# Two-layer decode forward and backward on one core: where layer 0's softmax numerators, two K chunks and a weight tile are kept, and when the output rows are written

## The chip, the cores and the metric

The kernel runs on one core of a Trainium2 chip. The metric is device time in microseconds (us) of one execution. Three runs of the kernel before took 1101.24, 1101.69 and 1105.03 us; the median is 1101.69. A fourth execution was profiled; its own time is given below.

The core has TensorE (PE, with its weight loads shown as PEld), VectorE (DVE), ScalarE (ACT), GpSimd (POOL) and SyncE (SP). Here SP issues the loads, POOL the stores, each in order. SBUF is addressed as 128 partitions; sizes below are elements per partition.

## What is computed

Two rounds of attention block and MLP over a KV cache, for one token in each of two batches, with one set of weights used by both rounds, and then the gradient of all inputs but one (`B_x`) for a given `grad_out`. Cut to what matters:

```
B, Sq, D = 2, 1, 1024;  Hq, Hkv, Sk, Dh = 32, 4, 16384, 128;  F = 3584

def A(x, k_cache, v_cache, wq, wo):
    q = (x @ wq).reshape(B, Sq, Hq, Dh).transpose(0, 2, 1, 3)
    k, v = repeat(k_cache, 8, axis=1), repeat(v_cache, 8, axis=1)
    p = softmax(einsum("bhqd,bhkd->bhqk", q, k) * Dh ** -0.5)
    o = einsum("bhqk,bhkd->bhqd", p, v)
    return o.transpose(0, 2, 1, 3).reshape(B, Sq, Hq * Dh) @ wo

def Bm(x, w1, b1, w2, b2):
    return gelu(layernorm(x) @ w1 + b1) @ w2 + b2

def fwd(x, ...):                       # the same weights twice
    x = x + A(layernorm(x), ...);  x = x + Bm(layernorm(x), ...)
    x = x + A(layernorm(x), ...);  x = x + Bm(layernorm(x), ...)
    return x

out, vjp = jax.vjp(fwd, x, k_cache, v_cache, wq, wo, w1, b1, w2, b2)
return out, *vjp(grad_out)
```

`out_0` is the result and `out_1` the gradient of x (2 x 1024 each); `out_2` and `out_3` are the gradients of the two caches (32 MB each in bf16), `out_4` to `out_9` those of the weights and biases.

## The kernel before

**Units.** The cache has eight groups (two batches, four KV heads). A group's K, and its V, is four chunks; a chunk is one tile of 128x4096 bf16 (1024 KB), and a chunk is worked in four slots of eight 128x128 blocks. Weights come in tiles of the same size. The pool `ld` holds seven such tiles in turn; ten more tiles of that size have fixed places (`mid8`, `late8`, `keepV0` to `keepV3` and `keepK0` to `keepK3` for the last group, and `keepxV`, `keepxK`). What is in a fixed place is loaded once and used by later passes: `kv_load` (L518) keeps a table `held`, and `early` (L504) names tiles that stay until a phase: K chunk 2 of group 0 in `mid8` until layer 1's forward pass, V chunk 0 of group 0 in `late8` until layer 1's backward pass.

**Forward pass of a layer** (`attn_layer_fwd`, `attn_fwd`, L612). A slot transposes eight K blocks on PE (`emit_T`, L535), and a copy by ScalarE or VectorE (`evac_bf16`, the one with less charged work) moves them from PSUM into the ring `kT`, four tiles of 128x1024. Two slots later PE forms the scores. After a group's 16 slots come the maximum, then 16 exponentials on ScalarE (`ex`, L654) into `e_all`, a tile of 128x16384 for both layers with layer 0's and layer 1's numerators beside each other (per group: 64 pairs of blocks, 2 layers, 8 heads, 2), and then the products with V (`Acc.quad`, L571).

**Layer order.** Layer 0's attention and MLP, layer 1's attention and MLP (the MLP's w1 tiles fill all seven `ld` buffers and are kept), then backward: `weights_down(1)` (L990: w1's products, then the eight wo tiles through class `Back`), `attn_bwd(1)` (L716, 128 slots, in order of groups), w2's products, `weights_down(0)`, and then the main loop from L1628 on, which does layer 0's attention backward and both layers' cache gradients. `Back.load` (L399) issues a tile's load and queues four units that turn it; `Back.run` turns tile k+1, then multiplies tile k.

**The main loop.** Each step m has two slots that transpose V blocks into the ring `kT`, scores against them, cache gradients (`kv_pair`, L1443: four products into four PSUM banks, four copies, a store) and units from two queues, `fill` and `late` (outer products of the weight gradients; `step_fill`). Operands come as blocks (`make_blks`, L1216: transposed numerators and score gradients) and as spread queries (`q_spread`, `q_make`). The operands of the first chunks are made ahead, in a function that `weights_down(0)` calls after its third w1 tile (`mid`), together with the row of `out_0`: `col_to_row_f32` (L201) turns the eight f32 columns with f32 transposes in one PSUM bank, in two halves, and stores 2 x 1024. The same function writes `out_1` in the tail, behind the last layer-norm backward (`attn_in_bwd`), between the last two `kv_pair` calls.

**Rings.** Besides the transposed K, `columns` (L302) takes a tile of the ring `kT` for the transposed sums at the end of each `Back`. The order on each engine is the order in which the program is written; the framework adds the semaphore waits.

Of the kernel before, what the change touches and what calls it, by code (L numbers as in the profile page):

```python
# [23 lines left out]
def kernel(  # L24
# [60 lines left out]
    ktp = ctx.enter_context(tc.tile_pool(name="ktp", bufs=4))  # L85
# [115 lines left out]
    def col_to_row_f32(colT, J, dram_out, name, home, queue=nc.gpsimd):  # L201
        row = home[0:2].rearrange("p a b -> p (a b)")
        for j0 in range(0, J, 4):
            ps = pm_([2, 4, 128], F32, name)
            for j in range(4):
                PE.transpose(ps[0:2, j, :], colT[:, j0 + j, :], identf[:])
            V.tensor_copy(out=row[:, j0 * 128:(j0 + 4) * 128], in_=ps[0:2, :, :].rearrange("p a b -> p (a b)"))
        queue.dma_start(dram_out, row[:, :])
# [93 lines left out]
    def columns(acc, fin, start=True):  # L302

        n = acc.shape[-1] // 32
        xt = ktp.tile([128, 8, 128], BF16, name="xt", tag="kT")
        x = xt[:].rearrange("p a b -> p (a b)").bitcast(F32)[:, 0:n * 32]
        V.transpose(out=x, in_=acc)
        xv = x.rearrange("p (n m) -> p n m", m=32)
        for q in range(4):
            PE.matmul(fin[32 * q:32 * q + 32], lhsT=fold[:], rhs=xv[:, :, 2 * q:2 * q + 2], start=start, stop=True,  # L310
                      tile_position=(0, 32 * q), skip_group_check=not start)
# [18 lines left out]
    def w_take(W, j0, nj, c0, cw):  # L330
        wt = ld.tile([128, LDW], BF16, name="wt", tag="ld")
# [44 lines left out]
    class Back:  # L376
# [22 lines left out]
        def load(self, k):  # L399
            j0, nj, c0, cw = self.tiles[k]  # L400
            wv = self.wv[k] = w_take(self.W, *self.tiles[k])
# [63 lines left out]
        def columns(self):  # L465
            if self.by_tile is not None:
                columns(self.acc[:, 0:32 * self.nd], self.p[:, :, 0:2], False)
# [19 lines left out]

    mid8 = res.tile([128, LDW], BF16, name="mid8")
# [7 lines left out]

    blkv_homes = [mid8[:, 3584:4096], late8[:, 512:1024]]
# [6 lines left out]
    early = {("K", 0, 2): (mid8, 1), ("V", 0, 0): (late8, 2)}  # L504
# [30 lines left out]
    def emit_T(cv, b, third):  # L535
# [4 lines left out]
        kT = ktp.tile([128, 8, 128], BF16, name="kT", tag="kT")  # L540
        evac_bf16(kT[:].rearrange("p a b -> p (a b)"), tp[:].rearrange("p a b -> p (a b)"), 1024)
# [78 lines left out]
    def attn_fwd(l, q_bf, rbc, oT, groups, tail=lambda step: None):  # L620
# [10 lines left out]
        def post(g):  # L631
# [22 lines left out]
            def ex(f, h):  # L654
                half = NP // 2
                S.activation(out=e_all[:, g, f * half:(f + 1) * half, l, h, :],  # L656
# [16 lines left out]
            a = Acc(g, "V", lambda u: e_all[:, g, u, l].rearrange("p h t -> p (h t)"), finish, g % 2)  # L673
# [28 lines left out]
        while s < len(slots) + 2 or sch.busy():  # L702
# [7 lines left out]
            if 2 <= s < len(slots) + 2:  # L710
                score(s - 2)
            if s >= len(slots):
# [3 lines left out]
    def attn_bwd(l, do_bf, dqT, dn, groups, ahead):  # L716
# [84 lines left out]
        while s < len(slots) + 2 or sch.busy():  # L801
# [20 lines left out]
            if wq_q:  # L822
                wq_q.popleft()()
            s += 1
        assert not wq_q
# [139 lines left out]
    def mlp_out(l, fps):  # L965
        xn = vec.tile([128, DJ, 2], F32, name=f"xM{l}")
        V.tensor_tensor(out=xn[:], in0=fps, in1=b2T[:].to_broadcast([128, DJ, 2]), op=ALU.add)
        V.tensor_tensor(out=xn[:], in0=xn[:], in1=saved[f"m{l}"]["xT"][:], op=ALU.add)
# [20 lines left out]
    def weights_down(l, gT, name, mid=None, w1b=None):  # L989
# [12 lines left out]
        w1b.some(0)  # L1002
        w1b.run(mid)
        wob = Back(A_wo, HD, D, 16, [4, 5, 0, 1, 6, 2, 3, 7], "do")
        for k in range(NLD):
# [155 lines left out]
    def w2a_end():  # L1161
# [19 lines left out]
    attn_bwd(1, do1, dq1, dn1, [b * HKV + kv for kv in (0, HKV - 1, *range(1, HKV - 1)) for b in range(2)  # L1181
                                     if b * HKV + kv != G - 1], w2b)

    for k in range(NLD - 2, len(w2b.tiles)):
        w2b.load(k)

    copies_on("A")
    w2b.some(0)
    g2 = attn_in_bwd(1, g3, dnp1, lambda: w2b.some(1, 1), lambda: (w2b.bank_d(), w2b.some(1, 2)),
                     gM_all[:, 0:DJ, lsl(0)])  # L1190
    w2b.open(gM_all[:, 0:DJ, lsl(0)])
    w2b.bank_p()
    w2b.run()
    w2b.columns()
    w1b = w1_back()
    w1b.bank_p()
    copies_on(None)
    mlp_hidden_bwd(0, w2b.parts())
    x4 = mlp_out(1, fps[:, :, 0:2])
# [6 lines left out]

    by_read, by_store = deque(), deque()
    banks = {"tp": lambda: pt([128, 8, 128], BF16, "tpe")}

    def mtp():  # L1210
        return banks["tp"]()
# [30 lines left out]
    cols = {}  # L1242
    for w in "VK":
        cols[w] = vec.tile([128, G, 2, 8], BF16, name="cols" + w)
        for k in range(2):
            if w + str(k) != "V0":
                V.tensor_copy(out=cols[w][:, :, k, :], in_=saved["a%d" % k]["qT_bf" if w == "K" else "doT_bf"][:])
# [3 lines left out]
    nc.gpsimd.memset(spr["V"], 0.0)  # L1251
# [15 lines left out]
    def q_parts():  # L1267
        q_spread("K", cols["K"][:, g0_].rearrange("p l r -> p (l r)"), 0, 16)
        q_make("K", g0_, px([128, 512], F32, "qk0"))
        q_spread("V", cols["V"][:, g0_, 1, :], 8, 8)  # L1270
        V.tensor_copy(out=wide_do[g0_][:, 8:16, 3], in_=cols["V"][:, g0_, 1, :])
# [4 lines left out]
    for i, g in enumerate(order):  # L1276
        wide_do[g] = do_tiles[i % 2]
    dq0 = vec.tile([128, G, 8], F32, name="dqT0")
# [3 lines left out]
    g1, dops = weights_down(0, g2, "0", lambda: (col_to_row_f32(x4, DJ, out_0.rearrange("b s d -> (b s) d"), "o0",  # L1282
# [351 lines left out]
    m = 0  # L1634
# [109 lines left out]
```

## Time and profile before

| what | value |
|---|---|
| median of three runs | 1101.69 us (1101.24 to 1105.03) |
| the profiled execution, its own time | 1098.26 us |
| its span, first to last instruction | 1096.4 us |
| mean granted TensorE clock | 0.875 |
| PE / PEld busy | 899.0 us (82%) / 661.2 us (60%) |
| DVE / ACT / POOL busy | 611.6 us (56%) / 531.2 us (48%) / 69.0 us (6%) |
| moved by DMA | 438.68 MB, mean 400 GB/s |
| HBM read / written | 337.66 MB / 98.58 MB |
| chain that ended last | PE 48%, DMA 32%, DVE 11%, issue 5%, ACT 3% |

How to read it: the page of the profile shows one execution. Busy time is summed over the span; the row of slices shows the span in 40 equal parts of 27.4 us. A line of windows gives, for a stretch, the busy time of each engine with its number of instructions in brackets, the clock granted to PE as a share of full speed, the busy share of the DMA engines and the rate that they moved. The chain of waits goes back from the last instruction to what released it; its lines are start, length and what ran, or which transfer was waited for. In groups and timelines a line names the source line, the engine, the operation and out<-in.

The stages of the profiled execution, by the lines in the timeline: layer 0's attention to about 180 us, its wo and MLP to 246; layer 1's attention 250 to 418, w1 to 434; `weights_down(1)` to 470; `attn_bwd(1)` 471 to 620; w2 to 652; `weights_down(0)` to 692; main loop to about 1075, tail to 1096.

### The profile page before, as it was taken

What the parts mean: (1) busy time and instruction counts of PE and PEld (TensorE: products, weight loads), DVE (VectorE), ACT (ScalarE), POOL (GpSimd) and SP (SyncE); (2) the same over time, 40 slices, a digit from 0 to 9 for tenths busy, and PEclk for the clock granted to TensorE, in tenths of its full rate; (3) what the DMA queues carried; (4) which work ended last, traced back from release to release, by engine and by line L of the source; (5) the groups of instructions that cost most, each with busy time, mean ns of one, the idle gap of its engine ahead of it and who ended that gap; (6) DMA issues with size and microseconds to landing.
All of it is one profiled execution on the core that took longest, in us unless ns stands there. A gap on an engine that the chain in (4) does not pass through costs nothing.

```text
span 1096.4 us, 37939 instructions
## 1 busy us (share of the span) xinstructions
PE 899.0 (82%) x16707; PEld 661.2 (60%) x16707; DVE 611.6 (56%) x1324; ACT 531.2 (48%) x1352; POOL 69.0 (6%) x122
## 2 busy tenths in 40 slices
PE   3979896466989886889987787789898897999896
PEld 3867675356777665777765676556555454445452
DVE  1544443062455445445343456579798676787776
ACT  0534443002645340333432334478688675686774
POOL 0000000000000000000000000022111111111210
PEclk9987977556999886999998989999999788797998
DMA  8999999999999997999999999998999999999997
GB/s 370 422 426 424 423 425 417 405 404 424 396 424 424 425 393 301 351 392 419 377 420 421 398 397 360 392 343 331 419 415 422 422 420 424 409 398 421 422 423 304
DMA packets 99540, 438.68 MB, mean 400 GB/s; under 512 B 7078, under 2 KB 10150, under 8 KB 62640
## 3 DMA queue, kind: packets, MB, share of 16 engines
q1 hardware_dynamic: 82032, 343.98, 77.9%
q0 software_dynamic: 17344, 92.29, 20.4%
q8 instruction: 130, 2.13, 0.7%
q14 instruction: 34, 0.28, 0.1%
HBM read 337.66 MB, written 98.58 MB: 398 GB/s over the span
## 4 chain that ended last, share of the span: by engine, by line
PE 48%; DMA 32%; DVE 11%; issue 5%; ACT 3%; POOL 0%; DVEq 0%; SPq 0%; POOLq 0%; ACTq 0%
PE tp L539 11%; DMA kv_V<-in_A_v_cache_dram 8%; DMA wt<-in_B_w_dram 5%; DMA kv_K<-in_A_k_cache_dram 5%; PE acc_all L571 5%; PE tpm L1651 4%; DMA wt<-in_A_wo_dram 4%; PE xm L1460 4%; PE sc L694 3%; DMA out_dram<-keepK 3%; PE xm L1374 2%; PE dp L1513 2%; PE wtp L373 2%; DMA keepK<-in_A_v_cache_dram 2%; PE dp L791 2%
## 5 line engine op out<-in xcount | busy, mean ns | idle before, releaser
L161 ACT COPY kT<-tp 128x512 int32<-128x512 int32 x201 | 118.0, 587 | 281.8 <-PE tp L539 268.7
L164 DVE COPY kT<-tp 128x1024 bf16<-128x1024 bf16 x167 | 114.2, 690 | 132.7 <-PE tp L539 122.1
L539 PE MATMUL tp<-ident,kv_K 128*128 128x128 bf16 x1664 | 138.4, 232 | 4.9 <-DMA kv_K<-in_A_k_cache_dram 4.6
L539 PEld LDWEIGHTS <-kv_K 128*128 128x128 bf16 x1664 | 105.1, 103 | 6.2 <-DMA kv_K<-in_A_k_cache_dram 5.5
L1460 PE MATMUL xm<-late,mid 64*128 64x512 bf16 x504 | 89.8, 407 | 8.8 <-ACT keepK L169 2.9
L172 DVE CAST big<-xm 128x512 bf16<-128x512 f32 x133 | 86.3, 684 | 16.7 <-PE xm L1460 11.3
L169 ACT CAST big<-xm 128x512 bf16<-128x512 f32 x151 | 82.2, 595 | 21.1 <-PE xm L1460 10.3
L694 PEld LDWEIGHTS <-kT 128*128 128x128 bf16 x2048 | 76.0, 98 | 27.1 <-issue 22.3
L694 PE MATMUL sc<-qT_bf,kT 128*128 128x8 bf16 x2048 | 91.7, 171 | 0.4 <-issue 0.4
L339 PEld LDWEIGHTS <-wt 128*128 128x128 bf16 x1920 | 57.4, 104 | 53.8 <-DMA wt<-in_B_w_dram 16.0
L169 ACT CAST keepV<-xm 128x512 bf16<-128x512 f32 (+1 forms) x137 | 75.0, 594 | 27.9 <-PE xm L1460 16.6
L656 ACT ACTIVATE e_all<-sc,negm 128x64 bf16<-128x64 f32 x256 | 77.1, 341 | 1.1 <-DVE negm L651 1.0
L161 ACT COPY wt<-wtp 128x512 int32<-128x512 int32 x70 | 38.5, 588 | 80.4 <-PE wtp L373 76.9
L172 DVE CAST keepV<-xm 128x512 bf16<-128x512 f32 (+1 forms) x101 | 65.8, 684 | 20.1 <-PE xm L1460 13.4
L539 PE MATMUL tp<-ident,kv_V 128*128 128x128 bf16 x832 | 67.7, 228 | 4.3 <-DMA kv_V<-in_A_v_cache_dram 4.0
L272 DVE STREAM_TRANSPOSE wt<-wt 128x512 int32<-128x512 int32 x106 | 64.0, 672 | 6.1 <-PE w2b_f L339 5.6
L571 PE MATMUL acc_all<-kv_V,e_all 128*16 128x256 bf16 x832 | 44.7, 295 | 24.6 <-DVE acc_all L554 12.8
L169 ACT CAST keepK<-xm 128x512 bf16<-128x512 f32 x98 | 52.9, 595 | 13.5 <-PE xm L1460 6.9
L656 ACT ACTIVATION_READ_ACCUMULATOR e_all<-sc,negm 128x1 f32 x256 | 59.3, 232 | 0.0
L539 PEld LDWEIGHTS <-kv_V 128*128 128x128 bf16 x832 | 53.2, 101 | 5.9 <-DMA kv_V<-in_A_v_cache_dram 4.5
L1513 PE MATMUL dp<-wdo,kT 128*128 128x64 bf16 x896 | 51.8, 204 | 0.0
L172 DVE CAST keepK<-xm 128x512 bf16<-128x512 f32 x69 | 44.7, 683 | 9.8 <-PE xm L1460 5.0
(373 smaller groups left out, 1498.9 us busy)
## 6 DMA issues: line engine op xcount, KB each, us to landing
kv_K<-in_A_k_cache_dram SPq DMA_DIRECT2D x79, 1024.0 KB, 12.9
kv_V<-in_A_v_cache_dram SPq DMA_DIRECT2D x78, 1024.0 KB, 11.5
wt<-in_B_w_dram SPq DMA_DIRECT2D x35, 1024.0 KB, 12.8
wt<-in_A_wo_dram SPq DMA_DIRECT2D x32, 1024.0 KB, 9.3
out_dram<-big POOLq DMA_DIRECT2D x26, 1024.0 KB, 17.7
out_dram<-keepV POOLq DMA_DIRECT2D x19, 1024.0 KB, 19.6
out_dram<-keepK POOLq DMA_DIRECT2D x17, 1024.0 KB, 17.6
wt<-in_A_wq_dram SPq DMA_DIRECT2D x16, 1024.0 KB, 11.2
```

Of the source, the lines that this page charges most:

```text
L161: S.copy(out=dst.bitcast(I32), in_=src.bitcast(I32))
L164: V.tensor_copy(out=dst, in_=src)
L169: S.copy(out=dst, in_=src)
L172: V.tensor_copy(out=dst, in_=src)
L272: V.transpose(out=w, in_=w)
L339: PE.matmul(fps[:, o0 + o, :].rearrange("p (a b) -> p a b", b=2), lhsT=wv[:, j, o * 128:(o + 1) * 128], rhs=x[:, j0 + j, :].unsqueeze(1).t ...
L539: PE.transpose(tp[:, j, :], cv[:, b * 8 + j, :], ident[:])
L571: PE.matmul(self.acc[cg:cg + 16, :], lhsT=coef(u), rhs=self.cv[:, t:t + 2, :].rearrange("p t d -> p (t d)"), start=False, stop=True, tile_ ...
L656: S.activation(out=e_all[:, g, f * half:(f + 1) * half, l, h, :], in_=sc[g][f][:, h, :].rearrange("p (a b) -> p a b", b=2), func=ACT.Exp, ...
L694: PE.matmul(sc[g][f][:, :, t % TH], lhsT=kT[:, j, :], rhs=q_bf[:, g, :], start=True, stop=True)
L1460: PE.matmul(pss[k][:], lhsT=blk[p:p + 64, o + 2 * h + k // 2, :], rhs=Qm[p:p + 64, :, :].rearrange("p a b -> p (a b)"), start=True, stop=T ...
L1513: PE.matmul(dp[:, :, t:t + 4], lhsT=kT[:, j, :], rhs=wd[:, :, x:x + 4], start=(b + j == 0), stop=False)
```

## The change

- **`e_all`.** Layer 0 writes its numerators compactly into the second half of `e_all` (`e_first(g)`: 1024 elements for each group), and its V products read them there. In layer 1's forward pass, at slots 10, 12, ... 24, GpSimd copies group after group to the places that `e_all` had before (`e_spread(g)`).
- **K chunks 0 and 1 of group 0** are loaded into the first half of `e_all`, which is free until then, and `early` keeps them there for layer 1's forward pass.
- **The ring of transposed K** becomes one tile `kt_all` of 128x4096 with four places handed out in turn (`kt_tile`), in place of a pool of four. In `weights_down(1)` it takes the first wo tile, whose load is issued ahead of w1's products; the other seven go through `ld` as before. `columns` for the kept w1 uses a place in `mid8`.
- **Rows.** `row_steps` makes two units of a row (four bf16 products with the identity each, into the banks that the caller names; the first half copied by ScalarE, the second by VectorE) and takes the place of `col_to_row_f32`. `out_0`'s row, now from bf16 columns, joins the queue `late` at step 12 of the main loop, with a ring place as its home; `out_1`'s halves stand after each half of the last V pair in the tail, and the units that were run between them now follow at the end. Copies go to ScalarE alone while the last layer-norm backward runs.
- **Operands.** Blocks, columns and spread queries of the first chunks move from `weights_down(0)` into six units (`ahead_units`) of `attn_bwd(1)`, one every four slots from 5/8 of its slots on.

```diff
-    def col_to_row_f32(colT, J, dram_out, name, home, queue=nc.gpsimd):
-        row = home[0:2].rearrange("p a b -> p (a b)")
-        for j0 in range(0, J, 4):
-            ps = pm_([2, 4, 128], F32, name)
-            for j in range(4):
-                PE.transpose(ps[0:2, j, :], colT[:, j0 + j, :], identf[:])
-            V.tensor_copy(out=row[:, j0 * 128:(j0 + 4) * 128], in_=ps[0:2, :, :].rearrange("p a b -> p (a b)"))
-        queue.dma_start(dram_out, row[:, :])
+    def row_steps(cols, J, dram_out, row, banks, queue):
+
+        def step(j0):
+            ps = banks()
+            for j in range(4):
+                PE.matmul(ps[0:2, j * 128:(j + 1) * 128], lhsT=cols[:, j0 + j, :], rhs=ident[:], start=True, stop=True)
+            dst = row[0:2, j0 * 128:(j0 + 4) * 128]
+            if j0 % 8 == 0:
+                S.copy(out=dst, in_=ps[0:2, 0:512])
+            else:
+                V.tensor_copy(out=dst, in_=ps[0:2, 0:512])
+            if j0 + 4 == J:
+                queue.dma_start(dram_out, row[0:2, 0:J * 128])
+        return [Unit(lambda j0=j0: step(j0)) for j0 in range(0, J, 4)]
...
+    kt_at = {"n": 0}
+
+    def kt_tile():
+        kt_at["n"] += 1
+        at = kt_at["n"] % 4 * 1024
+        return kt_at["home"][:, at:at + 1024]
...
+    half_e = G * NP * 16
+
+    def e_first(g):
+        return e_flat[:, half_e + g * NP * 16:half_e + (g + 1) * NP * 16].rearrange("p (u h t) -> p u h t", h=8, t=2)
+
+    def e_spread(g):
+        nc.gpsimd.tensor_copy(out=e_all[:, g, :, 0].rearrange("p u h t -> p u (h t)"),
+                              in_=e_first(g).rearrange("p u h t -> p u (h t)"))
+
-    early = {("K", 0, 2): (mid8, 1), ("V", 0, 0): (late8, 2)}
+    early = {("K", 0, c): (e_flat[:, c * LDW:(c + 1) * LDW], 1) for c in range(2)}
+    early |= {("K", 0, 2): (mid8, 1), ("V", 0, 0): (late8, 2)}
...
-            a = Acc(g, "V", lambda u: e_all[:, g, u, l].rearrange("p h t -> p (h t)"), finish, g % 2)
+            a = Acc(g, "V", lambda u: (e_first(g)[:, u] if l == 0 else e_all[:, g, u, l]).rearrange("p h t -> p (h t)"), finish, g % 2)
...
+            if l == 1 and s >= 10 and s % 2 == 0 and s < 10 + 2 * G:
+                e_spread((s - 10) // 2)
...
+            elif units and s >= len(slots) * 5 // 8 and s % 4 == 1:
+                units.popleft()()
...
         w1b.some(0)
+        wob = Back(A_wo, HD, D, 16, [4, 5, 0, 1, 6, 2, 3, 7], "do")
+        if l == 1:
+            wob.load(0, kt_all)
         w1b.run(mid)
-        wob = Back(A_wo, HD, D, 16, [4, 5, 0, 1, 6, 2, 3, 7], "do")
-        for k in range(NLD):
+        for k in range(l, NLD + l):
             wob.load(k)
...
+    ahead_units = deque([lambda: (nc.gpsimd.memset(spr["V"], 0.0), make_blks(0, None)), lambda: (cols_copy("K", 0), cols_copy("K", 1)),
+                         lambda: make_blks(1, None), lambda: cols_copy("V", 1), lambda: q_parts("K"),
+                         lambda: q_parts("V")])
...
-    g1, dops = weights_down(0, g2, "0", lambda: (col_to_row_f32(x4, DJ, out_0.rearrange("b s d -> (b s) d"), "o0",
-                                                                rows_home.rearrange("p (a b) -> p a b", b=128)),
-                                                 make_blks(0, None), make_blks(1, None), q_parts()), w1b)
+    g1, dops = weights_down(0, g2, "0", w1b=w1b)
...
+        if m == 3 * NCH:
+            late.extend(row_steps(x4[:], DJ, out_0.rearrange("b s d -> (b s) d"),
+                                  kt_tile(), mx, nc.gpsimd))
...
-    g0 = in_2()
+    copies_on("A")
+    in_2()
+    copies_on(None)
+    out_a, out_b = row_steps(out1, DJ, out_1.rearrange("b s d -> (b s) d"),
+                             kt_tile(), mx, nc.sync)
     kv_pair("V", i, 0)
-    step_fill(2)
-    col_to_row_f32(g0, DJ, out_1.rearrange("b s d -> (b s) d"), "o1", ktp.tile([128, 8, 128], BF16, name="o1", tag="kT"),
-                   nc.sync)
+    out_a()
     kv_pair("V", i, 1)
+    out_b()
```

## The prediction

> **What bounds the kernel now.** I read the row of slices first, then stretches of 10 us, then the chain of waits, then the DMA landings.
>
> ```profile
> DMA  8999999999999997999999999998999999999997
> GB/s 370 422 426 424 423 425 417 405 404 424 396 424 424 425 393 301 351 392 419 377 420 421 398 397 360 392 343 331 419 415 422 422 420 424 409 398 421 422 423 304
> ```
>
> Almost every slice has the DMA engines full, at about 424 GB/s where tiles are plain. So a microsecond is won in two ways: fewer bytes in a full stretch, or a gap made shorter. The gaps are slices 15 to 17 (the end of layer 1's forward pass and the start of its backward pass), 24 to 28, and the last one.
>
> ```profile
> core 0: us, PE busy (x) PEld busy (x) DVE busy (x) ACT busy (x) POOL busy (x), PEclk, DMA share, GB/s
> 270.00:280.00 10.00, 10.00 (x252) 9.94 (x250) 2.32 (x6) 8.92 (x16) 0.00 (x0) 1.00 1.01 424
> 360.00:370.00 10.00, 7.23 (x112) 5.71 (x110) 2.65 (x9) 1.76 (x3) 0.00 (x0) 0.70 1.01 425
> 430.00:440.00 10.00, 5.72 (x162) 5.37 (x163) 6.57 (x20) 2.50 (x5) 0.00 (x0) 0.67 0.20 70
> 660.00:670.00 10.00, 6.84 (x166) 5.61 (x162) 6.53 (x19) 4.36 (x9) 0.71 (x1) 1.00 0.98 331
> 860.00:870.00 10.00, 6.00 (x48) 3.41 (x45) 5.24 (x9) 4.85 (x10) 1.30 (x2) 0.78 1.01 422
> 1080.00:1090.00 10.00, 7.58 (x26) 2.36 (x25) 7.58 (x17) 5.47 (x11) 0.00 (x0) 0.66 0.60 241
> ```
>
> Layer 1's forward pass (250 to 432) starts with PE as the limit and is then held by DMA, with PE idle at 360. From 432 to 441 DMA has nothing to do: all seven `ld` buffers hold w1. At 660 DMA runs at 331 GB/s because compute returns buffers late. From 752 to 1075 DMA is full again while PE waits (860). At the end DMA falls to 241 GB/s and the engines set the time.
>
> ```profile
> 253.51 11.72 DMA kv_K<-in_A_k_cache_dram
> 420.06 13.92 DMA wt<-in_B_w_dram
> 456.81 8.61 DMA wt<-in_A_wo_dram
> 660.04 0.46 PE o L206 x4
> 660.52 0.69 DVE late L207
> 662.72 0.48 PE qk L1262 x4
> 1084.22 1.02 PE o L206 x4
> ```
>
> These are places on the chain that the change touches: layer 1's first K chunk, the last w1 tile, the last wo tile, the row and operand work inside w1's products, and the row of `out_1`.
>
> **The change, part by part.** Times are those of the profiled execution.
>
> *K chunks 0 and 1 stay in place.* Layer 1 loads five K tiles ahead of the first V tile in place of seven. Two loads of 1.049 MB at 424 GB/s are 2.47 us each, 4.95 us together, in a full stretch. PE gains less at first: its last q product ends at 263.90 and the first transpose waits until 265.28 for chunk 0, so it starts 1.4 us earlier. From there to about 300 PE is the limit and the ring of seven gives buffers back only as fast as PE reads. DMA, now two tiles ahead, can run dry (it already dips to 371 GB/s between 290 and 300). After 316 PE waits for V tiles (the chain has one of 11.0 us from 316.14) and is idle 2.8 us at 360, so it can use what DMA is ahead. The last w1 tile is issued at 420.06 and lands 13.92 us later, so the queue sets that end, not the issue. Bounds 1.4 and 4.95; a loss is excluded, since no load is added. The stretch is full for 130 of its 180 us, so I take 4.0.
>
> *Compact numerators.* Same activations (341 ns each) and products, other addresses: nothing. Eight GpSimd copies of 128x1024 bf16 are added at slots 10 to 24 of layer 1, about 271 to 284. The nearest row is a copy of the same length on 4 partitions, 1.04 us, so 8.3 us on an engine that is idle from 249 to 422. Layer 1's exponentials wait for a spread only from group 4 on, some 70 us later. VectorE copies beside that row keep their 0.69 us. Nothing lost if that holds; otherwise 8.3 us (a rival). The Trainium skill (GPSIMD Engine Reference, Specifications) says that GpSimd shares SBUF interfaces with VectorE, and contends with instructions in a 2-port mode or with two SBUF inputs. VectorE reads PSUM at 271 to 284, apart from tiny maxima, so by that rule too the cost is about nothing.
>
> *A wo tile in the transposed-K ring.* The first of eight wo tiles goes out right behind w1 into the gap at 432 instead of at 441, and the eighth no longer waits for a buffer from the first one's products (issue 456.81, landing 465.42). 2.5 us of transfer go into a gap. What is late next is VectorE: its sixteen stream transposes start at 455.9, 9.6 us of work to 465.5, then products of 1.5 us: about 467.2 instead of 469.8. The ring is idle between the passes, and slot 0's turn is over before the backward pass writes it. Bounds 1.0 (VectorE's waits shift only partly) and 2.7; I take 2.3.
>
> *Rows and operands leave w1's products in layer 0's backward pass.* Between 660.04 and 663.21 PE did eight f32 transposes, eight block transposes and four operand products, with waits for VectorE and ScalarE; the next weight turn starts at 663.2. That is 3.2 us of the chain. Lower bound 1.5, if DMA, which is nearly always busy there, cannot hurry; upper bound 3.9, what 650 to 690 (377, 331, 382, 384 GB/s) lacks against 408: 40 us x (1 - 368.5/408). I take 3.2.
>
> *Where they go.* Blocks, columns and operands: six units in layer 1's backward pass, slots 81 to 101 of 128, about 565 to 590: PE 1 us, ScalarE 1.3, VectorE 1.5, and an operand product that waits for VectorE (1.29 us for a like one at 824.67). DMA is full there (1.01 to 1.02) and PE is idle 1.2 to 3.7 us in each 10 us, so nothing; without that cover 2.5 us.
>
> *The row of `out_0`* becomes two units in the main loop (1.3 us on two engines, hidden under a full DMA), and its 4 KB store leaves from ring slot 2. That adds a wait: the built order has ScalarE's 38th copy into the ring of the main loop wait for that store.
>
> ```profile
> out_dram<-late POOLq DMA_DIRECT2D x1, 4.0 KB, 5.3
> out_dram<-keepV POOLq DMA_DIRECT2D x1, 2.0 KB, 17.6
> out_dram<-keepV POOLq DMA_DIRECT2D x1, 7.0 KB, 15.1
> ```
>
> ```profile
> 810.20 0.60 ACT L161 COPY kT<-tpm 128x512 int32<-128x512 int32 x1
> ```
>
> Alone, the row's store took 5.3 us; small stores behind 1 MB ones took 15.1 and 17.6, and that is its place now: issued near 809, wanted at 810.2. ScalarE would stand about 15 us. Behind it queue its PSUM copies, behind these PE's products (four banks), and the stores on POOL's queue. Cover: 1 MB stores of that moment land after 19 us, so DMA has 16 us and more to move, and PE's idle time from 860 to 950 lets compute catch up. Bounds 0 and 15; near full cover, so 2 us. By the Trainium skill (DMA: Bandwidth & Descriptors, Anatomy of one DMA) a DMA's fixed part is about 2 us, which would leave no stall worth pricing and a sum 2 us better; the two loaded rows speak against it here.
>
> *The end.* The row of `out_1` stops PE twice: f32 transposes, a VectorE copy, transposes again (1082.4 to 1085.2). With four bf16 products on rotating banks, each half between V pairs, that gap goes. From ln_bwd on, 22 copies of 0.59 to 0.69 us on two engines are 7.0 us, and the gradient comes 0.85 us earlier with ScalarE alone copying. From 1080.0 the copies end near 1087.3 where they ended at 1090.7; DMA is at 241 GB/s, so no limit. Some 0.6 us I give to banks: 2.8, bounds 1.5 and 4.0.
>
> *Sum:* 4.0 + 2.3 + 3.2 + 2.8 - 2.0 = 10.3 us. The profiled execution took 1098.26 us (span 1096.4 and 1.9 around it), so 1088.0; the median of the runs shown lies 3.4 us above it, so I forecast **1091.4 us**.
>
> **Rivals.**
> 1. *DMA was full anyway.* The wo tile and the 660 stall bring nothing, since DMA shows 0.98 to 1.07 at 650 to 690 and PE bounds 480 to 550 (9.5 us and more of 10). For it: these shares. Against: the rates beneath them. Left: 4.0 + 2.8 - 2.0 = 4.8 us: 1096.9. 15%.
> 2. *The row's store stops the main loop*: the slower side. One wait of ScalarE at the 38th ring copy, 15 us, up to 19 if the store waits out all that is queued. It decides when the DMA queue runs dry: uncovered by more than 12.3 us it eats all gains. At 15 us: 1101.69 - 12.3 + 15 = 1104.4, at 19 us 1108.4. For it: full load at 750 to 840, where the chain runs through engines. Against: store landings grow from 7.2 us (790) to 22 us (838), so compute is then faster than DMA. 12%.
> 3. *GpSimd's spread slows VectorE* by all of its 8.3 us at the PE-bound start: 1099.7. The 0.69 us copies beside a GpSimd copy speak against it. 4%.
> 4. *The main loop's new rotation of buffers* opens further dips like the 256 GB/s at 740 to 750, costing 7 to 10 us: about 1100. Nothing orders it either way. 9%.
>
> The loads counted in the built order exclude that the chunks are fetched again.
>
> **How the numbers follow.** The forecast holds 60%, with its own range 1086 to 1096: 15.5 us if all terms are at their best, 5.7 if DMA hides a part. Half a per cent, 5.5 us, is about what a measurement of this kernel can tell from no change. Faster than 1096.2: the forecast's 60%, 10 of rival 1's and 6 of the rest make 76%. Slower than 1107.2: rival 2's far end and two bad cases at once, 8%. Within: 16%. The 8-in-10 range leaves out the far end of rival 2 and a better sum than all terms: 1085 to 1101.
>
> **What would show it.** Right: K loads fewer by two and the w1 end at 430, not 434; DMA's empty stretch after it some 2.5 us shorter and no PE wait for the last wo tile; no row work inside w1's products and that stretch 3 us shorter; a ScalarE wait of 10 us and more in the main loop with DMA still near 420 GB/s; a tail without the double stop. Wrong: DMA dips before 316 as long as the two loads, or DMA under 350 GB/s after ScalarE's wait.

## The result, and the profile after

The changed kernel takes 1106.19 us (median of 20 runs, 1101.18 to 1113.49), the kernel before 1102.15 us (20 runs on the same chips, 1098.27 to 1106.45). The ratio is 1.0038, 95% interval 1.0024 to 1.0052: about 4 us slower. The forecast was 1091.4 us, so it is wrong by 14.8 us and in its sign.

The profiled execution of the changed kernel took 1112.88 us (span 1111.1), near the top of its runs; that of the kernel before, 1098.26 us, is at the bottom of its own. So the two traces say where time goes, and only the medians say how much. From the page of the changed kernel, the DMA engines' busy share and rate in 40 equal slices, and what was moved in all:

```profile
DMA  8999999999999997999999999979998899999997
GB/s 368 424 426 423 424 426 415 397 410 415 378 423 424 424 385 294 413 380 358 416 394 420 395 373 382 377 291 377 393 405 310 346 420 421 424 422 420 424 410 294
HBM read 335.56 MB, written 98.58 MB: 391 GB/s over the span
```

Before, 337.66 MB were read. So the two K chunks are spared, 2.1 MB or 4.95 us at 424 GB/s. The hole behind w1 is smaller: slices 15 and 16 move 294 and 413 GB/s, before 301 and 351. New holes are slices 30 and 31 (833 to 889 us, 310 and 346 GB/s), where the kernel before moved 422 in both. The same stretches of 10 us as in the prediction, and those around the new holes (each row: busy time and count of PE, PEld, DVE, ACT, POOL, then granted clock, DMA share, GB/s):

```profile
280.00:290.00 10.00, 8.69 (x202) 7.23 (x203) 4.54 (x8) 7.26 (x37) 0.00 (x0) 1.00 0.92 354
430.00:440.00 10.00, 6.04 (x181) 5.62 (x180) 5.58 (x18) 1.42 (x3) 0.00 (x0) 0.67 0.38 132
660.00:670.00 10.00, 6.42 (x183) 5.60 (x184) 4.42 (x8) 3.32 (x6) 0.00 (x0) 0.83 0.96 348
810.00:820.00 10.00, 4.14 (x53) 2.43 (x52) 5.12 (x9) 2.30 (x5) 1.11 (x2) 0.84 1.01 421
820.00:830.00 10.00, 0.87 (x8) 0.74 (x7) 0.00 (x0) 1.51 (x4) 0.00 (x0) 0.50 1.02 427
830.00:840.00 10.00, 9.13 (x86) 5.28 (x85) 6.06 (x10) 5.79 (x12) 0.53 (x1) 0.64 0.90 352
840.00:850.00 10.00, 8.63 (x78) 5.09 (x74) 6.66 (x18) 5.62 (x11) 1.60 (x3) 0.66 0.52 216
850.00:860.00 10.00, 9.37 (x90) 5.00 (x83) 6.68 (x11) 6.60 (x13) 0.77 (x1) 0.66 1.00 355
860.00:870.00 10.00, 9.17 (x118) 4.90 (x115) 8.80 (x15) 8.84 (x18) 1.60 (x3) 1.00 0.80 331
870.00:880.00 10.00, 9.66 (x110) 5.70 (x110) 7.88 (x14) 7.48 (x14) 1.83 (x3) 0.83 0.88 298
```

The kernel before, in two of these stretches:

```profile
820.00:830.00 10.00, 8.12 (x117) 5.28 (x117) 8.40 (x21) 7.49 (x15) 2.25 (x4) 1.00 1.02 428
840.00:850.00 10.00, 9.40 (x112) 5.58 (x109) 7.82 (x14) 7.96 (x15) 1.30 (x2) 0.83 1.02 419
```

In the changed kernel, between 820 and 830, the engines stand still (PE 0.87 us of 10, VectorE 0) while DMA runs full; the 50 us after it move 5.7 MB less than 424 GB/s would, 13.4 us of transfer. Who stood and for whom, in ScalarE's timeline of the changed kernel (start, length, line, operation, and in brackets the idle time before it and what ended it):

```profile
809.51 0.57 ACT L208 CAST kt_all<-xm 2x512 bf16<-2x512 f32 x1
828.49 0.59 ACT L160 COPY kt_all<-tpm 128x512 int32<-128x512 int32 x1 [15.71 <-DMA out_dram<-kt_all]
```

and in GpSimd's queue:

```profile
811.68 0.55 POOL L212 DMA_DIRECT2D out_dram<-kt_all  x1 [3.54 <-ACT keepV L168]
813.52 0.56 POOL L1370 DMA_DIRECT2D out_dram<-big  x1 [1.30 <-DVE acc_all L579]
830.84 0.53 POOL L1370 DMA_DIRECT2D out_dram<-keepV  x1 [16.75 <-ACT keepV L168]
```

ScalarE writes half of the row of `out_0` into the ring slot at 809.51, GpSimd issues its 4 KB store at 811.68, and the next copy into that slot waits 15.71 us for it to land. For 16.75 us no store is issued. Then the loads starve; from the waits of SyncE's queue between 811 and 880 (total, times, longest):

```profile
SPq L1439 <- DMA out_dram<-keepK: 29.6, 2, 16.2
```

A load needs a buffer, a buffer comes free when its store has landed, and the stores are 16 us late. SyncE waited for stores as long before (64.5 us in all in these 69, now 58.5; the longest single wait was 12.4). New is that DMA has too little else to do meanwhile: its busy share is 0.52 in 840 to 850, before 1.02.

Time of like VectorE instructions against the kernel before's trace (us, minus is earlier), by their place in that trace; the last column is the end of the span:

| kernel | 340 | 416 | 470 | 691 | 811 | 870 | 1079 | end |
|---|---|---|---|---|---|---|---|---|
| changed | -4.2 | -1.4 | -2.9 | -1.2 | +2.6 | +18.6 | +15.0 | +14.7 |
| row_own | -4.5 | -1.8 | -3.2 | -6.0 | -4.6 | -11.0 | -7.3 | -4.7 |
| row_only | +0.9 | +0.2 | -0.1 | +0.2 | +0.8 | +13.0 | +6.5 | +8.8 |
| a_only | -3.8 | -1.5 | -1.1 | +1.1 | +2.3 | +0.8 | +4.6 | +3.3 |

Each row is one execution. The changed kernel and row_own differ only in the row's place, used from about 805 us on, and yet by 4.8 us at 691; three kernels alike up to 430 us (row_own, own_tail, own_early) show -4.5, -2.7 and -2.2 at 340. So only the larger steps are read here, above all the 16 us between 811 and 870 in the changed kernel and the 12 in row_only (870 lies beside a wait of the kernel before, and instructions next to it read up to 8 us otherwise).

### The profile page after: what moved, and what is told of

It is laid out like the page before. It is cut to its first block, busy times and chain, and to the rows that moved or that the text cites. A ratio compares the mean times of both kernels' runs of the same rounds, so it can differ in the third digit from the quotient of the medians.

```text
span 1111.1 us, 37952 instructions
## 1 busy us (share of the span) xinstructions
PE 903.6 (81%) x16707; PEld 663.1 (60%) x16707; DVE 611.5 (55%) x1321; ACT 532.5 (48%) x1356; POOL 77.2 (7%) x130
## 4 chain that ended last, share of the span: by engine, by line
PE 39%; issue 16%; DMA 9%; DVE 7%; ACT 5%; POOL 0%; DVEq 0%; ACTq 0%; POOLq 0%; SPq 0%
PE tpm L1684 6%; PE xm L1493 5%; PE tp L564 4%; PE xm L1407 3%; PE dp L1546 3%; PE acc_all L596 2%; DMA kv_K<-in_A_k_cache_dram 2%; PE wtp L384 2%; PE dp L818 2%; DMA big<-in_A_v_cache_dram 2%; DMA out_dram<-kt_all 2%; PE tpm L384 1%; DVE wt L277 1%; ACT keepK L168 1%; DVE big L171 1%
## 5 line engine op out<-in xcount | busy, mean ns | idle before, releaser
L160 ACT COPY kt_all<-tp 128x512 int32<-128x512 int32 x200 | 117.4, 587 | 283.8 <-PE tp L564 273.8
L163 DVE COPY kt_all<-tp 128x1024 bf16<-128x1024 bf16 x168 | 114.9, 690 | 127.2 <-PE tp L564 114.8
L564 PE MATMUL tp<-ident,kv_K 128*128 128x128 bf16 x1536 | 123.7, 226 | 3.3 <-DMA kv_K<-in_A_k_cache_dram 3.0
L564 PEld LDWEIGHTS <-kv_K 128*128 128x128 bf16 x1536 | 92.9, 100 | 4.2 <-DMA kv_K<-in_A_k_cache_dram 3.4
L719 PE MATMUL sc<-qT_bf,kt_all 128*128 128x8 bf16 x2048 | 91.3, 171 | 0.2 <-issue 0.2
L719 PEld LDWEIGHTS <-kt_all 128*128 128x128 bf16 x2048 | 75.3, 97 | 26.4 <-issue 20.9
L350 PEld LDWEIGHTS <-wt 128*128 128x128 bf16 x1920 | 57.3, 103 | 52.5 <-issue 14.7
L168 ACT CAST keepV<-xm 128x512 bf16<-128x512 f32 (+1 forms) x121 | 65.6, 595 | 21.0 <-PE xm L1493 19.3
L168 ACT CAST keepK<-xm 128x512 bf16<-128x512 f32 x115 | 61.9, 596 | 18.3 <-PE xm L1493 10.0
L171 DVE CAST keepV<-xm 128x512 bf16<-128x512 f32 (+1 forms) x91 | 59.1, 684 | 16.7 <-PE xm L1493 13.5
L596 PE MATMUL acc_all<-kv_V,e_all 128*16 128x256 bf16 x832 | 44.2, 292 | 24.6 <-DVE acc_all L579 12.4
L171 DVE CAST keepK<-xm 128x512 bf16<-128x512 f32 x85 | 55.6, 685 | 10.7 <-PE xm L1493 7.7
L1546 PE MATMUL dp<-wdo,kt_all 128*128 128x64 bf16 x896 | 52.6, 206 | 0.0
## 6 DMA issues: line engine op xcount, KB each, us to landing
kv_K<-in_A_k_cache_dram SPq DMA_DIRECT2D x75, 1024.0 KB, 13.4
```

The lines of the kernel that those rows point to most:

```text
L160: S.copy(out=dst.bitcast(I32), in_=src.bitcast(I32))
L163: V.tensor_copy(out=dst, in_=src)
L168: S.copy(out=dst, in_=src)
L171: V.tensor_copy(out=dst, in_=src)
L564: PE.transpose(tp[:, j, :], cv[:, b * 8 + j, :], ident[:])
L596: PE.matmul(self.acc[cg:cg + 16, :], lhsT=coef(u), rhs=self.cv[:, t:t + 2, :].rearrange("p t d -> p (t d)"), start=False, stop=True, tile_ ...
```

## The experiments

Each kernel was timed beside the kernel before on the same chip. Median, ratio to before and 95% interval (the ratio is not the quotient of the two medians: for d_only that would be 0.9988):

| kernel | what it is | us | ratio | interval |
|---|---|---|---|---|
| row_own | changed, row of `out_0` in a place of its own | 1097.12 | 0.9948 | 0.9926 to 0.9970 |
| row_sp | changed, row's store issued by SyncE | 1097.17 | 0.9956 | 0.9940 to 0.9972 |
| row_only | before, only the row moved, into the ring | 1107.34 | 1.0054 | 1.0031 to 1.0076 |
| row_only_own | before, only the row moved, own place | 1099.46 | 0.9986 | 0.9970 to 1.0001 |
| a_only | before + step (a) | 1100.47 | 0.9978 | 0.9962 to 0.9994 |
| b_only | before + step (b) | 1100.86 | 0.9995 | 0.9979 to 1.0011 |
| ab | before + (a) + (b) | 1098.99 | 0.9973 | 0.9958 to 0.9988 |
| c_only | before + operands moved | 1101.57 | 1.0003 | 0.9983 to 1.0024 |
| d_only | before + new tail | 1100.35 | 1.0003 | 0.9987 to 1.0019 |
| own_mid | row_own, operands moved back | 1096.93 | 0.9947 | 0.9927 to 0.9967 |
| own_tail | row_own, old tail | 1098.75 | 0.9972 | 0.9954 to 0.9989 |
| own_early | row_own, another wo tile first | 1097.25 | 0.9965 | 0.9947 to 0.9983 |

Here (a) is the K chunks kept with the compact numerators, (b) the wo tile in the ring. Two kernels of the table that ran on different chips are best compared by their ratios; where medians are used below, the text says so.

**row_own: where the row lies.** Partitions 96 and 97 of `rowsA` are free until the end of the loop.

```diff
-                                  kt_tile(), mx, nc.gpsimd))
+                                  rowsA[96:98, 2048:3072], mx, nc.gpsimd))
```

> Theory S (slot): the changed kernel loses its time in the main loop, where ScalarE's copy into a ring slot waits 15.7 us for the small store of out_0's row that reads this slot, and TensorE stands 15.0 us behind it. With the row in a place of its own no TensorE wait above 6 us is left between 800 and 840 us, and the time is 4 to 9 us under the changed kernel's 1106.2 (1097 to 1102). Rival R (rotation): the loss comes from the main loop's other rotation of buffers, which this kernel keeps; then the time stays within 2 us of 1106, with transfers under 400 GB/s where the stall was.

From the trace of row_own, the row's store among the DMA issues (median us to landing last), and two of the stretches where the changed kernel had its hole:

```profile
out_dram<-rowsA POOLq DMA_DIRECT2D x1, 4.0 KB, 16.2
```

```profile
820.00:830.00 10.00, 7.85 (x97) 4.27 (x95) 8.16 (x21) 7.60 (x15) 1.30 (x2) 0.99 1.02 425
840.00:850.00 10.00, 9.29 (x119) 5.07 (x122) 9.36 (x16) 8.87 (x17) 1.83 (x3) 1.00 1.02 425
```

The store is as slow as before, 16.2 us, but nobody waits for it, and both holes are gone. Theory S holds: 9.1 us under the changed kernel by the medians (9.9 by the ratios; 4 to 9 were expected), and faster than the kernel before by 5.7 us (3.3 to 8.2).

**row_sp: why the store is late.**

```diff
-                                  kt_tile(), mx, nc.gpsimd))
+                                  kt_tile(), mx, nc.sync))
```

> Row in the ring slot as in the changed kernel, but its store issued by SyncE in place of GpSimd. Theory S1: the store lands late because it stands behind the 1 MB stores in GpSimd's queue; issued by SyncE it lands in under 8 us, ScalarE's wait falls under 5 us, time 1099 to 1103. Rival S2: all transfers of this stretch land late since the sixteen engines are full, whatever the queue; the wait stays 10 us or more, time 1104 to 1108.

ScalarE's timeline of row_sp (the store was issued at 806.15):

```profile
811.09 0.58 ACT L160 COPY kt_all<-tpm 128x512 int32<-128x512 int32 x1 [3.34 <-DMA out_dram<-kt_all]
```

Same slot, same 4 KB, same full DMA: 4.9 us to the copy in place of 16.7. The stores that GpSimd issued at that time, between 800 and 815 us, still land late:

```profile
out_dram<-big POOLq DMA_DIRECT2D x3, 1024.0 KB, 20.5
```

Theory S1 holds: the store waited behind the 1 MB stores of its own queue. That GpSimd's queue is slow by itself is excluded: the kernel before issues the row's store there at 662.87, with DMA full of loads (share 0.98) but nothing issued by GpSimd for 190 us, and it lands in 5.3 us. A wait of 3.3 us costs nothing that shows: the time is row_own's, 1.8 us under the 1099 to 1103 that were expected. This kernel also keeps the row's turn of the ring, which row_own drops, so that turn is not what costs. The Trainium skill (DMA: Bandwidth & Descriptors, Queues, rings and completion order) says that each queue has a ring on every DMA engine, that a ring is taken in order and that an engine turns between the rings it has work for. The two traces agree: 16.7 us behind GpSimd's stores, 4.9 us on SyncE's ring.

**row_only and row_only_own: the row alone.** The kernel before, with the row's two units in the main loop (as the changed kernel has them), once in a slot of the ring and once in `rowsA`. Both take the ring from one tile of four slots, and differ by this line:

```diff
-                                  kt_tile(), mx, nc.gpsimd))
+                                  rowsA[96:98, 2048:3072], mx, nc.gpsimd))
```

> The kernel before with only out_0's row moved into the main loop and into a ring slot (everything else as before). Theory S: a wait of ScalarE of 10 us or more for the row's store appears around 810 us, and the time rises by 3 to 10 us over the kernel before (1105 to 1112), since the removal from weights_down(0) gives back 1 us at most. Rival R: within 1.5 us of the kernel before.

> row_only (the kernel before with only out_0's row moved into the main loop) with the row in rowsA in place of a ring slot, that one address changed. Theory S: no TensorE wait of more than 6 us for a ring copy, time 1100 to 1102.5, that is 5 us or more under row_only's 1107.3 and 0 to 1.5 us under the kernel before (the row's share of step (c)). Rival R (what costs is the row's work in the main loop, wherever it lies): 1105 to 1108.

PE's longest wait between 690 and 1070 us in row_only, and the row's store in row_only_own:

```profile
PE tpm L1256 <- ACT kt_all L160: 17.3, 1, 17.3
```

```profile
out_dram<-rowsA POOLq DMA_DIRECT2D x1, 4.0 KB, 17.7
```

One address makes 7.9 us between the medians (7.5 by the ratios). Without any other part of the change the wait appears, 17.3 us long, and costs 5.9 us net of what leaving `weights_down(0)` gives. Rival R (the row's work itself) falls.

**ab, a_only, b_only: the parts that spare or advance loads.** Cut from the diff as it stands; the core of (a), and of (b) (ab has both):

```diff
-    early = {("K", 0, 2): (mid8, 1), ("V", 0, 0): (late8, 2)}
+    early = {("K", 0, c): (e_flat[:, c * LDW:(c + 1) * LDW], 1) for c in range(2)}
+    early |= {("K", 0, 2): (mid8, 1), ("V", 0, 0): (late8, 2)}
...
+        if l == 1:
+            wob.load(0, kt_all)
         w1b.run(mid)
-        for k in range(NLD):
+        for k in range(l, NLD + l):
```

> The kernel before with only the two parts that spare or advance loads: layer 0's numerators compact, K chunks 0 and 1 kept, and the wo tile in the ring. Theory L (lead): the 6.3 us of the prediction's sum can't be kept, because the loads run into a full ring while TensorE bounds attn_bwd(1), and the next stretch is bound by the transfers again; the changed kernel's lead is 2.9 us at 470 us and 1.2 us at 690 us, so the time is 0 to 2.5 us under the kernel before (1099.5 to 1102). Rival Q (the sum): 1095 to 1097.5, with a lead of 5 us or more at 690 us.

> The kernel before with compact layer-0 numerators, GpSimd's spreads and K chunks 0 and 1 kept in their place, nothing else. Step (a) of the prediction: 4.0 us faster than before (1097 to 1098.5). Theory L (lead lost where the ring is full and TensorE bounds): 0.5 to 2.5 us faster (1099.3 to 1101.3).

> The kernel before with the wo tile loaded into the ring before weights_down(1), nothing else. Step (b) of the prediction: 2.3 us faster than before (1099 to 1100). Theory L: 0 to 1.5 us faster (1100.3 to 1101.8).

(a) is worth 2.4 us (0.7 to 4.2), (b) 0.6 us (-1.2 to 2.3), both 3.0 us (1.3 to 4.6). Theory L's sizes hold for each alone; for both together it allowed 2.5 us at most. Its mechanism holds for (a) alone. The start of layer 1 in a_only:

```profile
270.00:280.00 10.00, 10.00 (x242) 9.81 (x240) 2.48 (x7) 8.85 (x16) 5.09 (x5) 1.00 0.98 388
280.00:290.00 10.00, 8.70 (x199) 7.21 (x196) 4.68 (x8) 6.89 (x36) 0.00 (x0) 1.00 0.93 356
290.00:300.00 10.00, 8.74 (x196) 7.42 (x195) 4.67 (x12) 4.91 (x18) 0.00 (x0) 1.00 0.99 358
```

and a wait of its SyncE queue in 262 to 305 us:

```profile
SPq L539 <- PE tp L550: 20.8, 5, 9.7
```

The same of the kernel before:

```profile
280.00:290.00 10.00, 8.69 (x197) 7.42 (x194) 4.15 (x7) 8.08 (x38) 0.00 (x0) 1.00 0.99 404
290.00:300.00 10.00, 8.74 (x192) 7.08 (x189) 4.09 (x12) 3.57 (x10) 0.00 (x0) 1.00 0.99 371
SPq L528 <- PE tp L539: 21.6, 7, 4.8
```

Before, these 30 us moved 424, 404 and 371 GB/s; now 0.97 MB less, which is 2.3 us of the 4.95 spared. The next load waits up to 9.7 us (before 4.8) for PE to give a buffer back. So part of DMA's lead is lost where PE sets the pace and every buffer is full; 2.6 us stay, and 2.4 are measured. The other traces agree: from 262 to 300 us the eight kernels with the kept chunks move 354 to 386 GB/s, the six without 397 to 406. The two that move least (ab 354, own_early 357) have the lowest granted clock of the eight there, 0.87 against 0.90 to 0.93. So what stays differs from execution to execution (ab's trace loses nearly all of it), and that 2.6 meets 2.4 is partly chance: by the table, VectorE's lead in a_only is 3.8 us at 340, 1.5 at 416 and gone at 691. The busy share hardly shows this shortage: 0.96 to 0.99 in 262 to 300 us (0.93 in ab and own_early), before 1.00.

For (b), the chain and VectorE's timeline of b_only:

```profile
446.45 9.50 DMA wt<-in_A_wo_dram
```

```profile
455.88 9.60 DVE L271 STREAM_TRANSPOSE wt<-wt 128x512 int32<-128x512 int32 x16
```

and of the kernel before:

```profile
455.89 9.59 DVE L272 STREAM_TRANSPOSE wt<-wt 128x512 int32<-128x512 int32 x16
```

The wait for the last wo tile (456.81, 8.61 us long before) is gone, but the sixteen transposes begin when layernorm's backward pass ends and fill 455.9 to 465.5 in both. Behind them the last tile's products begin at 466.70, before at 468.38. PE then stands after the first eight of 32, and the profile names nothing that it waits for; in b_only

```profile
468.45 0.76 PE L456 MATMUL do_p<-gA_all,wt 128*128 128x32 bf16 x24 [1.38 <-issue]
```

and before

```profile
469.03 0.76 PE L451 MATMUL do_p<-gA_all,wt 128*128 128x32 bf16 x24 [0.28 <-issue]
```

So of 1.7 us gained 1.1 are lost again, and the products end 0.6 us earlier.

**own_early: what binds behind the wo tile.**

```diff
-        wob = Back(A_wo, HD, D, 16, [4, 5, 0, 1, 6, 2, 3, 7], "do")
+        wob = Back(A_wo, HD, D, 16, [0, 4, 5, 1, 6, 2, 3, 7] if l else [4, 5, 0, 1, 6, 2, 3, 7], "do")
         if l == 1:
             wob.load(0, kt_all)
+            mid = lambda: wob.some(0)
```

> row_own with another tile of wo loaded first in weights_down(1): one that VectorE turns in place of one that TensorE turns, and VectorE turns it inside w1's products, at 440 to 450 us, where it has nothing to do. Theory V: step (b) failed since VectorE's 16 transposes of 0.67 us bind 455 to 465 us whatever arrives earlier; then VectorE's busy share there falls under 85% and the lead at 470 us over the kernel before grows by 1.5 to 2.7 us beyond row_own's 3.2, time 1094.5 to 1097. Rival T (the transfers bind there): no more lead at 470 us than row_own's, TensorE waits for a later tile of wo, time 1097 to 1099.

VectorE's timeline of own_early:

```profile
455.09 7.23 DVE L277 STREAM_TRANSPOSE wt<-wt 128x512 int32<-128x512 int32 x12
466.42 0.72 DVE L318 STREAM_TRANSPOSE kt_all<-do_d 128x512 f32<-128x512 f32 x1 [4.10 <-PE do_d L303]
```

and its chain:

```profile
445.64 9.52 DMA wt<-in_A_wo_dram
```

VectorE is done at 462.3, then waits 4.1 us for the products: theory V's share holds (VectorE 7.32 us of 455 to 465, where b_only has 9.89; but row_own, whose transposes begin earlier, has 8.07), its gain does not. From 436 to 470 us the lead grows by 0.4 us (from 0.3 to 0.7; row_own's stays at 3.3 and 3.2, so of the two leads at 470 only this growth can be compared), and the time is 1097.25, in theory T's range. So two paths of nearly one length lie there, VectorE's transposes and TensorE's products behind the wo loads; in the second, PE stands 1.67 us at the same place as in b_only, again with no wait named.

**c_only and own_mid: the operands.** c_only gives `ahead_units` to the kernel before and leaves the row in place; own_mid takes them back inside w1's products:

```diff
-                                     if b * HKV + kv != G - 1], w2b, ahead_units)
+                                     if b * HKV + kv != G - 1], w2b, deque())
...
-    g1, dops = weights_down(0, g2, "0", w1b=w1b)
+    def ahead_all():
+        while ahead_units:
+            ahead_units.popleft()()
+    g1, dops = weights_down(0, g2, "0", ahead_all, w1b=w1b)
```

> The kernel before with the four moved operand units taken from weights_down(0) into slots 81 to 101 of attn_bwd(1); out_0's row stays where it was. Step (c) of the prediction, without the row's share of it: 1.5 to 2.5 us faster (1099.5 to 1101). Rival C (weights_down(0) and the main loop are paced by transfers): within 1 us of the kernel before.

> row_own (the changed kernel with out_0's row in a place of its own), with the moved operands back inside weights_down(0)'s w1 products. Step (c) of the prediction: 3.2 us come back, 1099.5 to 1101 beside row_own's 1097.1. Rival C: weights_down(0) is paced by its weight loads and slots 81 to 101 of attn_bwd(1) pay for the moved work, so the time stays within 1.2 us of row_own (1096 to 1098.3).

c_only is 0.3 us slower than before (from 1.9 faster to 2.6 slower), own_mid 0.2 us faster than row_own by the medians: rival C, though c_only's interval reaches past its 1 us. From c_only, and the second stretch from the kernel before (its first is in the prediction):

```profile
660.00:670.00 10.00, 8.21 (x229) 6.78 (x226) 4.83 (x9) 4.25 (x9) 0.71 (x1) 1.00 0.96 334
670.00:680.00 10.00, 7.18 (x197) 6.43 (x198) 4.99 (x18) 4.80 (x11) 0.00 (x0) 1.00 1.01 372
```

```profile
670.00:680.00 10.00, 8.20 (x234) 7.46 (x235) 5.54 (x19) 4.46 (x9) 0.00 (x0) 1.00 1.07 382
```

With the operand work gone the rates are 334 and 372 GB/s, before 331 and 382. So the missing GB/s was not slack that this work caused; the share was 0.96 and 1.01 here, 0.98 and 1.07 before.

**d_only and own_tail: the end.** own_tail puts the old tail into row_own; d_only is the reverse, made on the kernel before:

```diff
-    copies_on("A")
-    in_2()
-    copies_on(None)
-    out_a, out_b = row_steps(out1, DJ, out_1.rearrange("b s d -> (b s) d"),
-                             kt_tile(), mx, nc.sync)
+    g0 = in_2()
     kv_pair("V", i, 0)
-    out_a()
+    step_fill(2)
+    col_to_row_f32(g0, DJ, out_1.rearrange("b s d -> (b s) d"), "o1", kt_tile().rearrange("p (a b) -> p a b", b=128),
+                   nc.sync)
     kv_pair("V", i, 1)
-    out_b()
```

> The kernel before with only the new tail for out_1's row. Step (d) of the prediction: 2.8 us faster than before (about 1099). Rival D (the last transfers set the end): within 1 us of the kernel before, with a later end of the last transfers behind an earlier last copy.

> row_own with the tail of the kernel before: float32 transposes of out_1's row in the single small bank, copies dealt between the engines. Step (d) of the prediction: 2.8 us slower than row_own (1099 to 1101), with 1.5 to 2 us more from the last layernorm sum to the last copy. Rival D: the end is set by the last transfers (one of the sixteen engines still moved some 25 GB/s for 6.8 us behind the others in row_own), and the time stays within 1.2 us of row_own.

d_only shows no gain (from 1.4 us faster to 2.1 slower); own_tail is 1.6 us slower than row_own by the medians, with intervals that overlap. The end of d_only:

```profile
1085.00:1090.00 5.00, 4.38 (x12) 1.35 (x10) 4.02 (x7) 3.77 (x7) 0.00 (x0) 0.71 0.70 281
1090.00:1095.00 5.00, 0.00 (x0) 0.00 (x0) 0.00 (x0) 0.11 (x1) 0.00 (x0) 0.63 0.57 221
1095.00:1099.00 4.00, 0.00 (x0) 0.00 (x0) 0.00 (x0) 0.00 (x0) 0.00 (x0) 0.50 0.05 20
```

From the last layernorm sum to the last copy it takes 8.6 us, before 10.0: 1.4 us are won. From the last copy to the end it takes 9.7 us, before 5.7. But own_tail, with the old tail, takes 8.3 and 9.8 us, row_own 8.6 and 10.4: the 1.5 to 2 us more to the last copy that were expected of it are not there, so the 1.4 us are one pair's and not shown to be the tail's. Whether (d) is worth nothing or some 2.6 us (the difference of the ratios of own_tail and row_own) stays open.

## Why the prediction was wrong, step by step

**The step that failed is the price of the row's store.** The prediction named the mechanism (the 38th copy, ScalarE, the slot, 15 us) and the trace has 15.71 us of wait and 15.0 us of PE behind it. It took 2 us from bounds of 0 to 15, "near full cover", since DMA had 16 us and more to move. DMA did stay full, at 421 and 427 GB/s, until 830. But the cover was a queue that the standing engines fill: no store was issued for 16.75 us, and one store's landing later the loads had no buffers. Its own sign of error, DMA under 350 GB/s after the wait, came at 840 (216 GB/s). Part of the hole is won back (before, PE was idle 15.2 us from 860 to 950, waiting for loads; in 880 to 970 of the changed kernel it is idle 8.6 us), and row_own prices the rest: 9.1 us between the medians, 7.1 more than the 2 taken. That is rival 2's mechanism, which was given 12%. That its 1104.4 to 1108.4 holds the result is luck: it sets 15 to 19 us against gains of 12.3, where the runs show 9.1 against 5.7. The landing time was right: the two loaded rows (15.1 and 17.6 us) foretold 16.7. The Trainium skill (DMA: Bandwidth & Descriptors, Anatomy of one DMA) gives a DMA issued by GpSimd a fixed part of about 2 us, whatever its size. No 4 KB store of a row on GpSimd's queue landed in that here: 4.5 to 5.3 us where no store stood ahead of it (before, a_only, b_only, ab, c_only, d_only), 16.2 to 19.1 us behind 1 MB stores.

**The savings were sized too high:** 12.3 us forecast (10.3 and the 2.0 taken off), 5.7 us in row_own. So 6.6 of the 14.8 us are theirs, nearly as much as the store's 7.1.
- (a) 4.0 forecast, 2.4 measured. The lower terms were seen ("DMA can run dry"), and the share kept was guessed from the length of the full stretch. The trace of before had the number: SyncE's queue waits 21.6 us of 262 to 305 for PE to give buffers back, and a lead meets that at once. The prediction's other sign of error, DMA dips before 316 as long as the two loads, came nearly in full in ab and own_early alone. The end of w1 came at 432.1 in the changed kernel and at 433.4 in a_only, not at 430, against 435.0 before.
- (b) 2.3 forecast, 0.6 measured. DMA's empty stretch shrank as forecast (132 GB/s in 430 to 440, was 70) and the wait for the last tile went. VectorE's transposes were named as next and end at 465.5 as forecast; the products of 1.5 us behind them are what failed. In b_only PE still turns the last tile until 466.2, stands 1.38 us inside the products, and ends them at 469.2 in place of 467.2.
- (c) 3.2 forecast. The operands bring nothing (c_only, own_mid), the row 1.5 us (-0.1 to 3.3, row_only_own). The mis-step: 368.5 of 408 GB/s was read as slack. Rival 1 read the shares instead and was right in the sizes of (b) and (c); for (b) it named PE's pace from 480 us on, while b_only has little to lose by then (0.6 us at 470).
- Moved operands in the backward pass: nothing forecast, nothing found. The change from 540 to 616 us is +0.1 us in c_only; by 619 it is +1.6, a jump that a_only, without these units, has too.
- (d) 2.8 forecast, 0 to 2.6 measured. d_only's engines are done 1.4 us sooner, own_tail's are not later; the kernel ends with transfers either way.
- The spreads were right. GpSimd's timeline of the changed kernel, the last five:

```profile
270.29 5.22 POOL L525 COPY e_all<-e_all 128x1024 bf16<-128x1024 bf16 x5 [0.26 <-ACT kt_all L160]
```

1.04 us each, as forecast, on an engine that was idle, and VectorE's stream is as long as before (2.32 us in 270 to 280 in both). The Trainium skill (GPSIMD Engine Reference, Specifications) names VectorE's work in a 2-port mode or with two SBUF inputs as what contends with GpSimd. This trace does not speak against it but hardly tests it: beside the eight copies VectorE runs one instruction, a maximum read from PSUM, 0.69 us long as before. Rival 3, 8.3 us lost, falls: a_only carries the spreads and is faster than before.
- Rival 4 (the new rotation) is not what costs: row_own keeps it and is faster than before. From 691 to 811 us row_own loses 1.4 us and the changed kernel, with the same rotation until the row, 3.8; a_only, with the old order, loses 1.2.

The terms measured alone add up to 2.4 + 0.6 + 1.5 and 0 to 2.6, or 4.5 to 7.1 us; row_own shows 5.7. The median of before used for the forecast, 1101.69, stood.

## What to carry to other kernels

A small output placed in a rotating buffer lends the buffer's next writer the landing time of its store, and that is set by what stands ahead in the issuing queue, not by its 4 KB: give it a place that nothing reuses, or another queue. A full DMA queue covers a stall only as long as the stalled engines do not feed it; count from the last store issued to the first load without a buffer. Price a saved transfer where buffers are free, and a saved wait by the second-longest path; a low rate at a busy share near 1 need not be slack: here it stayed when the work beside it was taken away.

## What the runs showed that was not expected

The last transfers end unevenly. After the last copies one stretch of row_own reads:

```profile
1085.00:1090.00 5.00, 0.00 (x0) 0.00 (x0) 0.00 (x0) 0.00 (x0) 0.00 (x0) 0.50 0.06 25
```

A share of 0.06 is that of one DMA engine of sixteen, at 25 GB/s, for some 6 us while the others are idle. It is there for 5 to 6 us in row_sp, row_only, own_mid, own_tail, own_early and d_only too, for some 4 in the changed kernel and under 2 in the kernel before; in a_only such a stretch of 3 us comes ahead of the last stores instead of behind them. What puts one engine behind was not tried. And the 4 KB store took 4.9 us through SyncE's queue and 16.2 to 19.1 us through GpSimd's at the same point of the program: the queue, and what stood in it, decided.

PE also seems to wait for its own instructions. The page of either kernel lists a queue of that kind (transfers, MB, share of the span):

```profile
q8 instruction: 130, 2.13, 0.7%
```

Five traces (before, changed, b_only, row_own, own_early) have 31 idle stretches of PE longer than 0.9 us for which the profile names nothing, the one that takes 1.1 us from (b) among them. All 31 end 2.2 to 2.4 us after a transfer of this queue, 16 KB each, begins. If that is what PE waits for, work that lets it run sooner gains less where such a transfer is next in line. No run changes these transfers, so the cause is not shown.
